# Token chunks of the second product taken from last to first, in a fused attention, experts and tanh-layer kernel on one core

## The chip, the cores and the metric

The kernel runs on one core of a Trainium2 chip. The metric is the time of one execution on the device in microseconds (us). In the profile, PE is TensorE (matrix products), PEld its weight loads, DVE is VectorE, ACT is ScalarE, POOL is GpSimd and SP is SyncE, which only issues DMAs here. Each of these engines takes its own instructions strictly in the order in which they stand in the program.

## The reference

Three layers follow one another; the output of one is the input of the next.

```python
# 1 attention: q, k, v are (2 batches, 8 heads, 576 positions, 64)
rel = pos[:, None] - pos[None, :]
mask_plain = (rel >= 0) & (rel < 32)                       # heads 0 to 3
mask_dil = (rel >= 0) & (rel < 128) & (rel % 4 == 0)       # heads 4 to 7
attn = softmax(where(mask, q @ k.T / sqrt(64), -1e9)) @ v
x = attn as (1152 tokens, 512)
# 2 four experts, all of them for every token
p = domain_probs / domain_probs.sum(-1)
for e in range(4):
    out += p[:, e:e + 1] * (relu(x @ w1[e]) @ w2[e])       # 512 -> 1024 -> 512
# 3 tanh layer, input: the out of layer 2
h = out @ w_in                                             # 512 -> 2048
out = (h - tanh(h)) @ w_out                                # 2048 -> 512
```

## The kernel before

**Precision.** A product of float32 numbers is made of three products of a faster 32-bit type: each operand is split into a high part, rounded by ACT, and a low part, the rest, by DVE or POOL. PE then adds high x high, high x low and low x high in PSUM.

**Stages and sets.** The hidden columns are cut into slices of 512: eight of the four experts (two each) and four of the tanh layer. The tokens are in two sets, set 0 of 512 tokens (four chunks of 128) and set 1 of 640 (five chunks). The list `seq` has 14 stages, each one slice with one or both sets. Stages 0 and 1 take set 0 alone, while the attention of set 1 is still being worked out beside them; stages 2 to 7 take both sets; stages 8 and 9 give set 1 the two slices that it missed; stages 10 (`N2`) to 13 (`LAST`) are the tanh layer with both sets.

**First product.** In stages 0 and 1 it is made directly (`whole`, L742, eight steps of 12 matmuls). From stage 2 on a scheme with seven products in place of eight is used, 14 steps of 6 matmuls for each stage and set (L803), listed in `ORDER`. Product P with its t (0 or 1) gives, after a few additions on DVE and POOL (L720), a half of one of the four hidden tiles `hts[g, f]`, f from 0 to 3: P2 gives half 0 of tile t, P3 half 1 of tile t, P7 half 1 of tile t + 2, and P4, the last, half 0 of tile t + 2. A half is half of the set's tokens: half 0 is the first 256 (or 320) of them.

**From product to hidden tile.** In expert stages ACT makes the high part with the relu (L723) and DVE the low part (L726). In tanh stages ACT takes the tanh (L774); for half 0 DVE subtracts, ACT makes the high part (L790) and DVE the low part (L128, into h); for half 1 DVE subtracts, ACT makes the high part (L165) and POOL the low part (L128, into h).

**Second product.** A chunk (`y_step`, L846) is 128 tokens x 512 outputs: for each f three matmuls, 12 in all, in one PSUM bank. `y_sum` then scales and adds it into `acc` (L867 in the experts, L876 in the tanh layer). Chunks are taken from the first tokens to the last. Before layer 3, `acc` is transposed on PE (L892).

**Order of the work.** The order is that in which the program emits the instructions, written out by hand. The list `steps` holds the products (`hs`) and chunks (`ys`) in PE's order; `start` gives each a scheduled time on a clock of its own. All other work is emitted through `when` and `later` with a due time on that clock. `merge(a, b, at)` puts the chunks `b` of the stage or set before between the products `a` at the places `at` (`FIRST`, `LATE` and `THEN`). `need(keys)` emits at once all work that is still pending under these keys; a chunk before asks for `("h", g)`, that is for all hidden tiles of its set.

**Other work in the stream.** Weights come by DMA and are split by ACT (L165) and POOL (L128). `w_in` and `w_out` are stored in another form and must be decoded by DVE, ACT, DVE and DVE again (L672, L676, L684, L689, with L683 on ACT), written back by DMA and loaded as weights later; 32 such decodes are spread by due times, nine of them in stages 11 and 12. The attention of set 1 is made during stages 0 to 2: scores on PE (L480), the masked maximum and the sums on DVE (L496, L502, L515 to L517), the multiplications on POOL (L503, L519), transposes on PE (L529, L542) and values on PE (L569); it is begun at due time 3 and repeated every `BEAT` = 11 for four pairs of heads; its result is then split into x operands (`prep`).

Of the kernel before, what the change touches and what calls it, by code (L numbers as in the profile page):

```python
# [26 lines left out]
SETS = [(0, 512), (512, 640)]  # L27
# [19 lines left out]
def _halves():  # L47
# [25 lines left out]
def tile_local_attention_moe_tanhshrink(  # L73
# [659 lines left out]
    def whole(n, f, half, kks=range(4)):  # L733
# [13 lines left out]
        if half == 1 and kks[-1] == 3:  # L747
            ht = hts[0, f] = h_tile(0)
            b, done = banks_.pop(f)
            later(0.0, lambda: relu(ht[:, 0], ht[:, 1], b, ("h", 0), done), ("h", 0))  # L750

# [13 lines left out]
    def hidden(n, g, f, half, b, done):  # L765

        Q = QH[g]
        hi, lo = (hts[g, f][:, i, half * Q:(half + 1) * Q] for i in range(2))
        key = ("h", g)
        if seq[n][0] < NS1:  # L770
# [22 lines left out]
    def product(n, g, P, t):  # L793
# [13 lines left out]

        later(0.0, lambda: sums_of(n, g, P, t, b, done), ("h", g))

    def sums_of(n, g, P, t, b, done):  # L810
# [19 lines left out]
        if P == 7:  # L830
            add(pt["u"], b, pt["u"])
        add(b, b, pt[{2: 1, 3: "u5", 7: "u5", 4: "u"}[P]])
        later(0.7, lambda: hidden(n, g, f, half, b, done), ("h", g))

    acc, oacc = {}, {}

    def y_step(n, g, c):

        need(("h", g), ("w2", n))
        y, done = f_bank()  # L840
        fs = range(NF)
        for f in fs:
            hh, hl = (hts[g, f][:, i, c * 128:(c + 1) * 128] for i in range(2))
            whi, wlo = (w2t[n, f][:, i] for i in range(2))
            for m, (a, b_) in enumerate(((hh, whi), (hh, wlo), (hl, whi))):
# [3 lines left out]
                )  # L849
        later(0.0, lambda: y_sum(n, g, c, y, done), ("y", n, g))  # L850

    def y_sum(n, g, c, y, done):
# [19 lines left out]
        else:  # L872
            k_ = 2 if n == LAST and ch == NCH - 1 else 1
            for i in range(k_):
# [50 lines left out]

    FIRST, LATE, THEN = (1, 2, 3, 4, 5), (4, 5, 6, 7, 8), (5, 7, 10, 13)
    steps = []
    for n in range(EARLY):
        steps += hs(n, 0) + ys(n, 0)
    steps += hs(EARLY, 0) + ys(EARLY, 0) + hs(EARLY, 1)  # L930
    for n in range(EARLY + 1, NS1):
        steps += merge(hs(n, 0), ys(n - 1, 1), FIRST) + merge(hs(n, 1), ys(n, 0), THEN)
    steps += ys(NS1 - 1, 1)
    for n in range(NS1, N2 - 1):
        steps += hs(n, 1) + ys(n, 1)
    steps += hs(N2 - 1, 1) + merge(hs(N2, 0), ys(N2 - 1, 1), LATE) + ys(N2, 0) + hs(N2, 1)
# [283 lines left out]
```

## Time and profile before

| | |
|---|---|
| median of 3 runs | 698.28 us (696.35 to 699.21) |
| the profiled execution | 698.15 us |
| its span, first to last instruction | 696.4 us |
| PE, DVE, POOL, ACT busy | 641.1, 452.2, 381.9, 291.7 us |
| mean granted clock of TensorE | 0.97 of full speed |
| matmuls | 4095 |

PE is busy for 92% of the span, the others for 42% to 65%. The profiled execution is 0.13 us under the median and lies between the runs, so its span can stand for the kernel; what it has beside the span is 1.75 us.

### The profile page before, as it was taken

How to read it: one execution, taken by the hardware profiler on the slowest of the kernel's cores; microseconds unless marked ns; L12 is line 12 of the kernel's file. 1: busy time of each engine (PE TensorE's matmuls, PEld its weight loads, DVE VectorE, ACT ScalarE, POOL GpSimd, SP SyncE). 2: the span in 40 equal slices, each digit the busy share in tenths (PEclk: the TensorE clock that was granted, in tenths of full speed). 3: DMA queues.
4: the chain of work that ended last, by engine and by line, in shares of the span. 5: the costliest groups of instructions: out<-in, count | busy, mean ns of one | idle time of the engine just before them, and what ended most of it. 6: DMA issues, size and time to landing. Idle time of an engine off the chain costs nothing.

```text
span 696.4 us, 10915 instructions
## 1 busy us (share of the span) xinstructions
PE 641.1 (92%) x4095; PEld 553.9 (80%) x4095; DVE 452.2 (65%) x859; ACT 291.7 (42%) x656; POOL 381.9 (55%) x352
## 2 busy tenths in 40 slices
PE   7876999999999999999999897999899968998997
PEld 3575878798888988978888787888698857986995
DVE  5575454655867867957948865754564883893662
ACT  2635545354433424324424444343674451652530
POOL 5466795373733814725625648584684860792520
PEclk9998999999999999999999999899999997998999
DMA  9951222003233234142151230523102233322012
GB/s 322 305 192 58 62 81 102 1 1 107 92 105 107 91 114 143 47 160 98 53 191 60 95 147 1 181 77 98 54 1 71 82 91 106 122 76 76 1 46 91
DMA packets 36693, 68.06 MB, mean 98 GB/s; under 512 B 4128, under 2 KB 10400, under 8 KB 36640
## 3 DMA queue, kind: packets, MB, share of 16 engines
q1 hardware_dynamic: 36640, 67.37, 28.9%
q8 instruction: 32, 0.52, 0.3%
q14 instruction: 21, 0.17, 0.1%
HBM read 56.61 MB, written 10.75 MB: 97 GB/s over the span
## 4 chain that ended last, share of the span: by engine, by line
PE 52%; DVE 24%; POOL 8%; issue 7%; DMA 4%; ACT 4%; SPq 0%; DVEq 0%; POOLq 0%; ACTq 0%
PE bank_f L846 21%; PE bank_f L803 12%; PE bank_s L846 8%; POOL w L128 4%; DVE h L726 3%; PE bank_a L846 3%; PE bank_s L803 3%; DVE single L689 3%; DVE single L676 2%; DVE single L684 2%; DVE single L672 2%; DMA double<-in_moe_w_out_dram 2%; DVE bank_f L720 2%; DMA in<-single 2%; PE bank_a L803 2%
## 5 line engine op out<-in xcount | busy, mean ns | idle before, releaser
L846 PE MATMUL bank_f<-w,h 128*128 128x512 f32 x876 | 223.2, 403 | 16.9 <-ACT h L790 8.0
L846 PEld LDWEIGHTS bank_f<-w,h 128*128 128x128 f32 x876 | 163.6, 193 | 56.4 <-ACT h L790 11.1
L128 POOL TENSOR_TENSOR w<-raw,w 128x512 fp32r<-128x512 f32 x110 | 145.2, 1326 | 108.3 <-ACT w L165 105.1
L803 PE MATMUL bank_f<-x,w 128*128 128x320 f32 (+1 forms) x1218 | 180.2, 300 | 4.4 <-DVE h L726 4.4
L803 PEld LDWEIGHTS bank_f<-x,w 128*128 128x128 f32 x1218 | 172.5, 191 | 10.2 <-DVE h L726 5.4
L720 POOL TENSOR_TENSOR sums<-u,p 128x320 f32<-128x320 f32 (+1 forms) x44 | 39.4, 899 | 97.0 <-DVE u L720 97.0
L846 PE MATMUL bank_s<-w,h 128*128 128x512 f32 x312 | 80.5, 408 | 5.6 <-ACT h L723 4.5
L165 ACT ACTIVATE w<-raw 128x512 fp32r<-128x512 f32 x112 | 68.7, 627 | 30.5 <-POOL raw L128 11.6
L846 PEld LDWEIGHTS bank_s<-w,h 128*128 128x128 f32 x312 | 60.0, 197 | 20.0 <-ACT h L723 5.4
L803 PE MATMUL bank_s<-x,w 128*128 128x320 f32 (+1 forms) x402 | 61.5, 298 | 1.5 <-DVE h L726 1.5
L803 PEld LDWEIGHTS bank_s<-x,w 128*128 128x128 f32 x402 | 57.2, 190 | 4.1 <-DVE h L726 2.2
L128 POOL TENSOR_TENSOR w<-sum,w 128x512 fp32r<-128x512 f32 x36 | 49.4, 1373 | 19.0 <-ACT w L165 19.0
L867 DVE SCALAR_TENSOR_TENSOR acc<-bank_f,pn,acc 128x512 f32<-128x512 f32 x43 | 32.1, 747 | 40.3 <-PE bank_f L846 40.0
L723 ACT ACTIVATE h<-bank_f 128x320 fp32r<-128x320 f32 (+2 forms) x83 | 35.0, 430 | 41.4 <-DVE bank_f L720 40.7
L726 DVE SCALAR_TENSOR_TENSOR h<-bank_f,h 128x320 fp32r<-128x320 f32 (+2 forms) x83 | 38.9, 474 | 13.7 <-ACT h L723 12.7
L683 ACT ACTIVATE double<-double 128x512 f32<-128x512 f32 x32 | 21.6, 676 | 56.7 <-DVE single L676 51.4
L676 DVE SCALAR_TENSOR_TENSOR single<-double,single 128x512 int32<-128x512 int32 x32 | 40.6, 1269 | 1.1
L815 ACT ACTIVATE p<-bank_f 128x320 f32<-128x320 f32 (+1 forms) x60 | 23.5, 418 | 37.7 <-PE bank_f L803 37.7
L165 ACT ACTIVATE w<-sum 128x512 fp32r<-128x512 f32 x36 | 22.7, 630 | 39.3 <-POOL sum L615 21.3
L689 DVE SCALAR_TENSOR_TENSOR single<-double,single 128x512 f32<-128x512 f32 x32 | 33.3, 1042 | 8.6 <-ACT double L683 7.9
L803 PE MATMUL bank_a<-x,w 128*128 128x320 f32 (+1 forms) x228 | 37.0, 298 | 1.0 <-DVE h L726 1.0
L803 PEld LDWEIGHTS bank_a<-x,w 128*128 128x128 f32 x228 | 33.3, 190 | 2.3 <-DVE h L726 1.3
(146 smaller groups left out, 838.0 us busy)
## 6 DMA issues: line engine op xcount, KB each, us to landing
raw<-in_moe_w_dram SPq DMA_DIRECT2D x40, 512.0 KB, 5.5
double<-in_moe_w_in_dram SPq DMA_DIRECT2D x16, 512.0 KB, 3.8
double<-in_moe_w_out_dram SPq DMA_DIRECT2D x16, 512.0 KB, 4.1
in<-single SPq DMA_DIRECT2D x16, 256.0 KB, 2.5
out<-single SPq DMA_DIRECT2D x16, 256.0 KB, 2.2
raw<-in SPq DMA_DIRECT2D x8, 512.0 KB, 5.6
raw<-out SPq DMA_DIRECT2D x8, 512.0 KB, 3.6
h<-in_v_dram SPq DMA_DIRECT2D x7, 512.0 KB, 8.6
```

Source lines behind the costliest of these rows:

```text
L128: engine.tensor_tensor(out=out, in0=a, in1=b, op=ALU.subtract)
L165: nc.scalar.activation(out=hi, in_=src, func=ACTF.Copy)
L676: nc.vector.scalar_tensor_tensor(out=t, in0=high, scalar=-0x40000000, in1=t, op0=ALU.bitwise_and, op1=ALU.bitwise_or)
L683: nc.scalar.activation(out=mag, in_=mag, func=ACTF.Square)
L689: nc.vector.scalar_tensor_tensor(out=w, in0=mag, scalar=HIGH_MIN * HIGH_MIN, in1=w, op0=ALU.is_ge, op1=ALU.mult)
L720: e.tensor_tensor(out=o, in0=x, in1=y, op=ALU.add)
L723: nc.scalar.activation(out=hi, in_=src, func=ACTF.Relu)
L726: nc.vector.scalar_tensor_tensor(out=lo, in0=src, scalar=0.0, in1=hi.bitcast(F32), op0=ALU.max, op1=ALU.subtract)
L803: nc.tensor.matmul(out=b, lhsT=w[:, wi, kk, t * 128:(t + 1) * 128], rhs=x[:, kk, xi, :], start=(kk == 0 and i == 0), stop=(kk == 1 and i = ...
L815: nc.scalar.activation(out=pt[P], in_=b, func=ACTF.Copy)
L846: nc.tensor.matmul(out=y, lhsT=a, rhs=b_, start=(f == 0 and m == 0), stop=(f == NF - 1 and m == 2),)
L867: nc.vector.scalar_tensor_tensor(out=t, in0=y, scalar=p, in1=t, op0=ALU.mult, op1=ALU.add)
```

## The change

1. **Chunks from the last tokens to the first.** `y_step` takes chunk 4 (or 3) first and chunk 0 last.
2. **A chunk asks only for the halves that it reads.** The pending work is filed under `("h", g, f, half)`, the fifth product's sum under `("u5", g, t)`.
3. **The first two chunks of a stage in two steps** (`direct`), in stages 0, 1, 2, 8 and 10. In stages 0 to 1 the first two chunks use f 0 to 2, and f 3 after both. In the other stages the first chunk's f 0 and 1 stand ahead of the last product; behind it come f 0 and 1 of the second chunk, and then f 2 and 3 of both.
4. **Places of chunks between products.** `LATE` goes from (4, 5, 6, 7, 8) to (3, 4, 5, 6, 8); in stages 12 and 13 (1, 2, 3, 4, 5) becomes (2, 3, 4, 5, 6).
5. **Decodes in stages 11 and 12.** Their stretch on the schedule's clock was the stage from 8 after its start to its end (39 of 47 in stage 11); now it is from 4 after its start to 8 before its end (35). Five decodes stand 7.0 apart in place of 7.8 in stage 11, and four 8.75 in place of 9.75 in stage 12; the first comes 4 earlier, the last some 7 earlier.
6. **Attention of set 1** begins at due time 9 in place of 3, with `BEAT` 10.5 in place of 11.

```diff
+MAKES = {
+    1: lambda t: (), 5: lambda t: (), 6: lambda t: (), 2: lambda t: (t, 0), 3: lambda t: (t, 1),
+    7: lambda t: (t + 2, 1), 4: lambda t: (t + 2, 0),
+}
...
-        key = ("h", g)
+        key = ("h", g, f, half)
...
-        later(0.0, lambda: sums_of(n, g, P, t, b, done), ("h", g))
+        later(0.0, lambda: sums_of(n, g, P, t, b, done), ("h", g, *MAKES[P](t)))
...
-    def y_step(n, g, c):
-
-        need(("h", g), ("w2", n))
-        y, done = f_bank()
-        fs = range(NF)
+    def y_step(kind, n, g, i):
+        c = SETS[g][1] // 128 - 1 - i
+        first = 3 if n < EARLY else 2
+        fs = {"y": range(NF), "ya": range(first), "yb": range(first, NF)}[kind]
+        if n < EARLY:
+            need(*[("h", g, f) for f in fs])
+        else:
+            halves = {c * 128 // QH[g], (c * 128 + 127) // QH[g]}
+            need(*[("h", g, f, half) for f in fs for half in halves])
+        need(("w2", n))
+        y, done = opened.pop((g, c)) if kind == "yb" else f_bank()
+        if kind == "ya":
+            opened[g, c] = y, done
...
-    FIRST, LATE, THEN = (1, 2, 3, 4, 5), (4, 5, 6, 7, 8), (5, 7, 10, 13)
+    def direct(h, n, g):
+
+        cs = ys(n, g)
+        (a0, b0), (a1, b1) = [[(kind, *step[1:]) for kind in ("ya", "yb")] for step in cs[:2]]
+        if n < EARLY:
+            return h + [a0, a1, b0, b1] + cs[2:]
+        return h[:-1] + [a0] + h[-1:] + [a1, b0, b1] + cs[2:]
+
+    FIRST, LATE, THEN = (1, 2, 3, 4, 5), (3, 4, 5, 6, 8), (5, 7, 10, 13)
...
-        steps += hs(n, 0) + ys(n, 0)
-    steps += hs(EARLY, 0) + ys(EARLY, 0) + hs(EARLY, 1)
+        steps += direct(hs(n, 0), n, 0)
+    steps += direct(hs(EARLY, 0), EARLY, 0) + hs(EARLY, 1)
...
-        steps += hs(n, 1) + ys(n, 1)
-    steps += hs(N2 - 1, 1) + merge(hs(N2, 0), ys(N2 - 1, 1), LATE) + ys(N2, 0) + hs(N2, 1)
+        steps += direct(hs(n, 1), n, 1)
+    steps += hs(N2 - 1, 1) + direct(merge(hs(N2, 0), ys(N2 - 1, 1), LATE), N2, 0) + hs(N2, 1)
...
-        first = FIRST if n > N2 + 1 else LATE
+        first = (2, 3, 4, 5, 6) if n > N2 + 1 else LATE
...
-            a += 8.0
+            a, b = a + 4.0, b - 8.0
...
-    BEAT = 11.0
+    BEAT = 10.5
...
-        due = 3.0 + BEAT * n
+        due = 9.0 + BEAT * n
...
-        when(BEAT * 3 + 20.0 + 4.0 * c, lambda c=c: prep(1, c, True, nc.vector, nc.gpsimd), ("x", 1, False))
+        when(BEAT * 3 + 25.0 + 3.0 * c, lambda c=c: prep(1, c, True, nc.vector, nc.gpsimd), ("x", 1, False))
```

The numbers of instructions do not change. Lines move a little: L742 is L747 in the changed kernel, L803 is L809, L846 is L865, L529 is L534, L480 is L485, L876 is L896, L672, L676, L684 and L689 are L677, L681, L689 and L694, L720 is L725, and L128 is L133.

**PE at the end of stage 0, before.** `w` and `h` with their numbers are the second weights and the hidden tiles of f 0 to 3 in this order; `att` is the second set's attention.

```order
L742 MATMUL bank_f<-x_532,w_226 128x256 x6
L529 MATMUL bank_a<-ident,att 96x128 x4
L846 MATMUL bank_f<-w_622,h_637 128x512 x3
L846 MATMUL bank_f<-w_638,h_702 128x512 x3
L846 MATMUL bank_f<-w_680,h_750 128x512 x3
L846 MATMUL bank_f<-w_703,h_798 128x512 x3
L529 MATMUL bank_a<-ident,att 96x128 x4
L480 MATMUL bank_s<-x_151,x_145 64x96 x20
```

The same place in the changed kernel:

```order
L747 MATMUL bank_f<-x_532,w_226 128x256 x6
L865 MATMUL bank_f<-w_622,h_637 128x512 x3
L865 MATMUL bank_f<-w_638,h_676 128x512 x3
L865 MATMUL bank_f<-w_658,h_717 128x512 x3
L865 MATMUL bank_f<-w_622,h_637 128x512 x3
L865 MATMUL bank_f<-w_638,h_676 128x512 x3
L865 MATMUL bank_f<-w_658,h_717 128x512 x3
L865 MATMUL bank_f<-w_677,h_777 128x512 x6
L865 MATMUL bank_f<-w_622,h_637 128x512 x3
L865 MATMUL bank_f<-w_638,h_676 128x512 x3
L865 MATMUL bank_f<-w_658,h_717 128x512 x3
L865 MATMUL bank_f<-w_677,h_777 128x512 x3
L534 MATMUL bank_a<-ident,att 96x128 x4
```

The transposes of the attention (L529) stood between the last product and the first chunk, and again behind it; now three whole chunks stand ahead of the first of them, and 18 matmuls ahead of the first use of the fourth hidden tile.

**PE at the end of stage 8, before.** L803 is the end of the first product; `h_0_1` to `h_3_1` are the four hidden tiles of set 1.

```order
L803 MATMUL bank_f<-x_1585,w_4294 128x320 x12
L846 MATMUL bank_s<-w_4441,h_0_1_4515 128x512 x3
L846 MATMUL bank_s<-w_4462,h_1_1_4528 128x512 x3
L846 MATMUL bank_s<-w_4477,h_2_1_4516 128x512 x3
L846 MATMUL bank_s<-w_4501,h_3_1_4529 128x512 x3
```

The same place in the changed kernel:

```order
L809 MATMUL bank_f<-x_1618,w_4307 128x320 x6
L865 MATMUL bank_f<-w_4441,h_0_1_4515 128x512 x3
L865 MATMUL bank_f<-w_4462,h_1_1_4528 128x512 x3
L809 MATMUL bank_s<-x_1618,w_4307 128x320 x6
L865 MATMUL bank_s<-w_4441,h_0_1_4515 128x512 x3
L865 MATMUL bank_s<-w_4462,h_1_1_4528 128x512 x3
L865 MATMUL bank_f<-w_4477,h_2_1_4516 128x512 x3
L865 MATMUL bank_f<-w_4501,h_3_1_4529 128x512 x3
```

Six matmuls of the first chunk stand ahead of the last product, which is six of the former twelve, and six of the second chunk between it and the tiles f 2 and f 3.

**DVE at the end of stage 11, before.** L720 and L128 into `bank` or `h` make the hidden tiles f 2 and f 3 of set 1, half 0; L876 adds a chunk; L672, L676, L684 and L689 are one decode.

```order
L672 TENSOR_SCALAR single<-double 128x512
L676 SCALAR_TENSOR_TENSOR single<-double,single 128x512
L876 TENSOR_TENSOR acc<-bank_f,acc 128x512
L684 SCALAR_TENSOR_TENSOR single<-double,single 128x512
L128 TENSOR_TENSOR h_2_1_5829<-bank_a,h_2_1_5829 128x320
L720 TENSOR_TENSOR bank_f<-bank_f,u 128x320
L689 SCALAR_TENSOR_TENSOR single<-double,single 128x512
L128 TENSOR_TENSOR bank_f<-bank_f,sums 128x320
L128 TENSOR_TENSOR h_3_1_5860<-bank_f,h_3_1_5860 128x320
```

The same place in the changed kernel:

```order
L896 TENSOR_TENSOR acc<-bank_f,acc 128x512
L133 TENSOR_TENSOR h_2_1_5836<-bank_a,h_2_1_5836 128x320
L725 TENSOR_TENSOR bank_f<-bank_f,u 128x320
L133 TENSOR_TENSOR bank_f<-bank_f,sums 128x320
L133 TENSOR_TENSOR h_3_1_5869<-bank_f,h_3_1_5869 128x320
L896 TENSOR_TENSOR acc<-bank_f,acc 128x512
L896 TENSOR_TENSOR acc<-bank_s,acc 128x512
L677 TENSOR_SCALAR single<-double 128x512
L681 SCALAR_TENSOR_TENSOR single<-double,single 128x512
```

The decode stood ahead of the low parts of the last two tiles; now they stand ahead of a decode. On PE at this place one product of the next stage stood ahead of the first chunk, and two stand there now.

## Rows read from the trace of the kernel before

**Rows 1.** The page: PE's busy time; the granted clock in 40 slices, in tenths.

```profile
PE 641.1 (92%) x4095; PEld 553.9 (80%) x4095; DVE 452.2 (65%) x859; ACT 291.7 (42%) x656; POOL 381.9 (55%) x352
...
PEclk9998999999999999999999999899999997998999
```

**Rows 2.** Windows: length, PE PEld DVE ACT POOL busy, granted clock, DMA share, GB/s.

```profile
41.50:134.60 93.10, 80.94 (x740) 69.43 (x737) 56.82 (x109) 44.21 (x97) 60.53 (x57) 0.96 0.21 68
...
427.37:440.00 12.63, 8.80 (x27) 6.64 (x26) 7.72 (x14) 4.37 (x10) 8.91 (x7) 0.73 0.03 4
489.88:498.08 8.20, 6.54 (x28) 4.50 (x26) 4.51 (x9) 4.97 (x14) 7.08 (x8) 1.00 0.19 64
566.48:584.18 17.70, 9.62 (x34) 7.06 (x33) 10.77 (x20) 5.64 (x13) 7.70 (x7) 0.71 0.47 149
625.45:638.10 12.65, 9.62 (x32) 7.12 (x31) 5.67 (x10) 4.20 (x10) 3.97 (x4) 0.73 0.32 105
```

**Rows 3.** Windows of four stretches at half clock, same columns.

```profile
53.30:60.00 6.70, 2.92 (x9) 2.51 (x10) 6.36 (x14) 4.44 (x11) 3.27 (x4) 0.50 0.07 26
432.20:438.90 6.70, 6.15 (x15) 4.77 (x16) 5.66 (x10) 2.06 (x4) 3.90 (x4) 0.50 0.00 0
572.10:582.20 10.10, 5.37 (x16) 4.18 (x16) 6.16 (x10) 2.71 (x6) 2.17 (x2) 0.50 0.45 139
630.10:636.90 6.80, 5.64 (x16) 4.75 (x17) 1.68 (x3) 1.20 (x4) 0.12 (x1) 0.50 0.47 149
```

**Rows 4.** Timeline of PE: start, length, instruction, idle time before and its releaser.

```profile
57.08 1.09 PE L529 MATMUL bank_a<-ident,att 128*96 128x128 f32 x4 [8.13 <-POOL att L519]
...
134.63 1.62 PE L803 MATMUL bank_f<-x,w 128*128 128x320 f32 x10
```

**Rows 5.** Timeline of DVE in stages 0 and 1.

```profile
47.04 0.65 DVE L496 SCALAR_TENSOR_TENSOR att<-bank_s,mask_True 128x480 f32<-128x480 f32 x1
...
57.23 0.68 DVE L726 SCALAR_TENSOR_TENSOR h<-bank_f,h 128x512 fp32r<-128x512 f32 x1
...
130.51 0.48 DVE L128 TENSOR_TENSOR x<-xf,x 128x320 fp32r<-128x320 f32 x1
```

**Rows 6.** Timeline of PE, stages 3 to 6: first and last of four waits.

```profile
200.00 1.03 PE L846 MATMUL bank_a<-w,h 128*128 128x512 f32 x3 [0.70 <-ACT h L723]
...
348.97 1.03 PE L846 MATMUL bank_s<-w,h 128*128 128x512 f32 x3 [0.70 <-ACT h L723]
```

**Rows 7.** Timeline of DVE at the end of stage 8.

```profile
430.13 0.49 DVE L726 SCALAR_TENSOR_TENSOR h<-bank_f,h 128x320 fp32r<-128x320 f32 x1 [3.17 <-ACT h L723]
```

**Rows 8.** Timeline of PE from the end of stage 11 on.

```profile
575.20 0.79 PE L846 MATMUL bank_f<-w,h 128*128 128x512 f32 x1 [3.09 <-DVE h L128]
...
580.36 3.83 PE L846 MATMUL bank_s<-w,h 128*128 128x512 f32 x12
584.02 0.87 PE L803 MATMUL bank_s<-x,w 128*128 128x256 f32 x6
...
588.19 2.91 PE L846 MATMUL bank_f<-w,h 128*128 128x512 f32 x12
590.94 0.88 PE L803 MATMUL bank_f<-x,w 128*128 128x256 f32 x6
591.65 0.63 PE L846 MATMUL bank_f<-w,h 128*128 128x512 f32 x2
```

**Rows 9.** Timeline of POOL: low parts of hidden tiles at the ends of stages 11 and 12.

```profile
571.95 1.04 POOL L128 TENSOR_TENSOR h<-x,h 128x320 fp32r<-128x320 f32 x1
...
627.68 1.31 POOL L128 TENSOR_TENSOR h<-x,h 128x320 fp32r<-128x320 f32 x1
```

**Rows 10.** The decodes: two on DVE's timeline, then the tile's durations, min/median/max in ns.

```profile
561.40 0.67 DVE L672 TENSOR_SCALAR single<-double 128x512 int32<-128x512 int32 x1 [1.69 <-DMA in<-single]
...
571.50 0.78 DVE L672 TENSOR_SCALAR single<-double 128x512 int32<-128x512 int32 x1 [0.84 <-DMA in<-single]
...
L676 DVE SCALAR_TENSOR_TENSOR single<-double,single x32: 691/1658/1669, 149.8 to 623.2; 128x512 int32<-128x512 int32 x32
```

More of the change, by code (lines that the diff above doesn't have):

```diff
@@ L749, in whole @@
             b, done = banks_.pop(f)
-            later(0.0, lambda: relu(ht[:, 0], ht[:, 1], b, ("h", 0), done), ("h", 0))
+            key = ("h", 0, f)
+            later(0.0, lambda: relu(ht[:, 0], ht[:, 1], b, key, done), key)
     store, ring = [], {"u5": 0, "th": 0}
@@ L821, in sums_of @@
             add(u, b, pt[1])
-            later(0.5, lambda: add(u5, u, p5, nc.gpsimd), ("h", g, t, "u5"))
+            later(0.5, lambda: add(u5, u, p5, nc.gpsimd), ("u5", g, t))
             done()
             return
-        f, half = {2: (t, 0), 3: (t, 1), 7: (t + 2, 1), 4: (t + 2, 0)}[P]
+        f, half = MAKES[P](t)
         if P == 2:
@@ L828, in sums_of @@
         if P in (3, 7):
-            need(("h", g, t, "u5"))
+            need(("u5", g, t))
         if P == 7:
@@ L832, in sums_of @@
         add(b, b, pt[{2: 1, 3: "u5", 7: "u5", 4: "u"}[P]])
-        later(0.7, lambda: hidden(n, g, f, half, b, done), ("h", g))
+        later(0.7, lambda: hidden(n, g, f, half, b, done), ("h", g, f, half))
     acc, oacc = {}, {}
-    def y_step(n, g, c):
-        need(("h", g), ("w2", n))
-        y, done = f_bank()
-        fs = range(NF)
+    opened = {}
+    def y_step(kind, n, g, i):
[11 more added lines that the diff above has]
+            opened[g, c] = y, done
         for f in fs:
@@ L849, in y_step @@
                 )
-        later(0.0, lambda: y_sum(n, g, c, y, done), ("y", n, g))
+        if kind != "ya":
+            later(0.0, lambda: y_sum(n, g, c, y, done), ("y", n, g))
     def y_sum(n, g, c, y, done):
@@ L872, in y_sum @@
         else:
-            k_ = 2 if n == LAST and ch == NCH - 1 else 1
+            k_ = 2 if n == LAST and g == 1 and c == 0 else 1
             for i in range(k_):
@@ L944, in duration @@
             return 2.73
+        if kind in ("ya", "yb"):
+            return 2.73 * ((3 if n < EARLY else 2) if kind == "ya" else (1 if n < EARLY else 2)) / 4
         if n < EARLY:
@@ L951, in tile_local_attention_moe_tanhshrink @@
         start[step] = END
+        if step[0] == "yb":
+            start[("y", *step[1:])] = END + duration(*step) - 2.73
         END += duration(*step)
     def emit_step(kind, n, g, i):
-        if kind == "y":
-            y_step(n, g, i)
+        if kind[0] == "y":
+            y_step(kind, n, g, i)
         elif n < EARLY:
```

## The prediction

> **What bounds the kernel now.** I read the page first, for which engine is full: PE is busy 641.1 of 696.4 us of span, the others far less, and its clock dips in single slices only [rows 1]. So PE's work sets the time, and since the change neither adds nor removes an instruction, all that it can win is PE's idle time and PE's work at half clock. Then PE's waits, and a window around each: five stretches hold most of what the change touches [rows 2]. PE is idle there for 93.10 - 80.94 = 12.16 us (stages 0 and 1 and what follows), 3.83 (end of stage 8), 1.66 (start of stage 10), 8.08 (end of stage 11) and 3.03 (end of stage 12). In four of them the granted clock fell to 0.50, the lower of its two levels, after or in an idle time, and PE did 2.92, 6.15, 5.37 and 5.64 us of its work so [rows 3]. The rate without waits is seen in a chunk at full clock: 590.94 - 588.19 = 2.75 us for 12 matmuls, 0.229 each, and 591.65 - 590.94 = 0.71 for a product of set 0 [rows 8]. What a stretch loses is its length less its work at these prices.
>
> **Stages 0 and 1.** After stage 0's last product PE waits 8.13 us in front of the attention's transposes, for POOL [rows 4]; behind them stands the first chunk. In the changed order the chunk comes first and waits for the low part of f 2, which DVE ends at 57.23 + 0.68 = 57.9 [rows 5]. From before that instruction DVE loses two maskings of 0.65 [rows 5], two reductions of the same size, estimated as long, and a sum with its two small followers, estimated at 1.0: 3.6 together, so f 2 is ready at 54.3. PE is free at 57.08 - 8.13 = 48.95, and waits 5.3. The 18 matmuls that come next (4.1 us) cover f 3. Idle time and half clock lose 12.16 + 2.92/2 = 13.6 now; 8.3 is won, and I take 0.8 off because the clock may still fall after 5.3 idle: **-7.5**. Best case -13.6. Worst case: the attention's end moves later in order, and set 1's x operand is its last link. DVE ends it at 130.51 + 0.48 = 131.0 [rows 5], and set 1's products start at 134.63 [rows 4], a margin of 3.6. Its last part is due 2.5 later (56.5 + 3 against 53 + 4). If this chain doesn't come ahead with PE, all but 1.1 of the gain is waited away: -1.1. POOL is busy 60.53 of 93.10 in this window [rows 2], so the chain has room to come ahead.
>
> **Stages 3 to 6.** Four waits of 0.70 for the relu of the last half [rows 6]. The chunk that comes first now reads half 1, which the last product doesn't make: **-2.8** (best -2.8, worst half of it, -1.4).
>
> **Stage 8.** The 24 matmuls from 427.37 to 440.00 would take 5.5 at the full rate; 7.1 is lost. The first six now go ahead of the last product (estimated at 0.88 from 0.71 by its 320 columns), from 426.5 on. But the high part of f 1 comes only at 430.1, where DVE's wait for it ends [rows 7]; ACT is what is late, not the product's place. So PE waits some 2.9 after f 0, and then has 0.69 + 0.88 + 4.1 to do: 435.8, at best -4.2. If the 18 matmuls run at half clock as now, 4.1 of that goes: -0.1. Between the two I take **-2.3**.
>
> **Stage 10.** From 489.88 to 498.08 the two first chunks take 8.20 [rows 2], 2.7 more than 24 matmuls. Their f 2 and 3 now come behind 12 matmuls that need neither; an estimated 0.4 is left: **-2.3** (best -2.7, worst 0).
>
> **End of stage 11.** From 566.48 to 584.02 PE does 24 matmuls and a product, 6.2 us; 17.54 - 6.2 = 11.3 is lost. One of its waits, 3.09, is for the low part of a half 0 [rows 8], behind decode steps of up to 0.78 and 1.66 on DVE [rows 10]. The new first chunk reads half 1 alone, whose last low part POOL ends at 571.95 + 1.04 = 573.0 [rows 9]. PE, with one more product ahead and nine matmuls of f 0 to 2, gets there at 566.48 + 0.71 + 2.06 = 569.25; two of the three matmuls of f 3 don't need the low part, so 3.75 - 0.46 = 3.3 of wait stays. 11.3 - 3.3 = 8.0, less 1.0 for a few matmuls at half clock: **-7.0**. Best -11.3; worst -3, if only the product (0.71) and the decode's two steps (2.4) are won.
>
> **End of stage 12.** The same: 12.65 - 6.2 = 6.4 is lost. POOL's low part ends at 627.68 + 1.31 = 629.0 [rows 9], PE gets there at 625.45 + 2.77 = 628.2; 0.3 stays, and 0.6 for the clock: **-5.5** (best -6.4; worst, by the share 3.0 of 8.0 of the stage before, -2.3).
>
> **Other places.** The keys and the split of the last chunk move a few tenths: **-0.5** (best -1.5; worst +0.6, because the chunk that is summed last is now the one that is transposed first).
>
> **Decodes.** They cost DVE the same work; their place behind the tiles is counted above. Price of the closer spacing: two start 571.50 - 561.40 = 10.1 apart now, and DVE stood 0.84 and 1.69 for the DMA of the one before [rows 10]. Such a wait hides as long as PE has products whose sums come later, and gets longer if decodes come every 7.0. **+2.0**, an estimate of some 0.2 for each of nine; best 0. The second decode step takes 0.69 at least and 1.66 in the median [rows 10], so at worst nine go from the short to the long: 9 x 0.97 = +8.7.
>
> The Trainium skill (SBUF - State Buffer, "Who interferes with whom") says that a DVE instruction with two inputs in SBUF and a GpSimd instruction that reads SBUF exclude each other for their whole length. That second step has both inputs in SBUF, and the trace agrees that it has two lengths; that the page's lock is the cause, no row here shows. By the rule, decodes moved beside POOL's weight splits would all be slow, as in the fifth rival below.
>
> **Sum.** -7.5 - 2.8 - 2.3 - 2.3 - 7.0 - 5.5 - 0.5 + 2.0 = -25.9, against the profiled execution's 698.15 us (0.13 below the median of the runs): **672**. All bounds at their best -42.4 or 656; all at their worst +1.4 or 699.6.
>
> **Rivals.**
> 1. Set 1's x operand becomes the wait, at 127 to 134: early term -1.1, time 672.2 + 6.4 = 679. For it: the later due. Against: POOL's idle 32.6 in the window. Chance 0.13.
> 2. POOL's low parts hold the first chunks of stages 12 and 13's turn as long as DVE and ACT did: those two terms at their worst, + 7.2, time 679. For it: half 1 goes through POOL alone, behind its weight splits; against: both rows end before PE's present waits do. Chance 0.14.
> 3. All waits and half clocks at these places go: 656. Against: rows 7 name ACT for stage 8, which the change leaves. Chance 0.08.
> 4. DVE's decodes become a chain through the DMA: 5 x (10.1 - 7.0) + 4 x (10.1 - 8.75) = 20.9 in place of 2.0, time 691. For it: DVE waits for that DMA already. Against: 10.1 holds schedule time stretched by PE's own waits, and the waits were 1.69 and 0.84 only. Chance 0.07.
> 5. The moved decodes' second steps all take the long form: +8.7 in place of 2.0, 679. Against: the median shows that most do so already. Chance 0.04.
> 6. Slower: in the tanh stages the first chunk of every set (eight of them) now reads half 1 through POOL, where it read half 0 through DVE. If each waits there, the 14.8 of stages 10 to 12 isn't won (687), and from 11.1/8 = 1.4 per place on the kernel is slower; with two of POOL's 1.31 in front of each it is 687 + 21 = 708. Against: POOL is busy 7.70 of 17.70 and 3.97 of 12.65 there [rows 2], far from full. Chance 0.04.
> 7. The waits only move, each to the next instruction that needs the same tile: about 698. Against: in stages 11 and 12 the tiles themselves are ready earlier. Chance 0.04.
>
> **How the numbers follow.** The forecast as worked out has 0.46. The range of 660 to 688 holds it and rivals 1, 2 and 5, and 1 and 2 together (686); rivals 4, 6 and 7 and most of 3 are left out, 0.2 or a little more. A change of 0.5%, 3.5 us, is about what a measurement of this kernel tells from none: faster 0.92, within it 0.04 (rival 7), slower 0.04 (rival 6).
>
> **What the changed profile would show.** PE's first gap after stage 0's last product some 5 us and released by DVE's low part of a hidden tile, no longer by POOL's attention; set 1's first products near 127. No 0.70 waits in stages 3 to 6. At the end of stage 8 a wait of about 3 before f 1, for ACT. At the ends of stages 11 and 12 one wait each, of 3 and under 1 us, for POOL's low part of half 1, and shorter stretches at half clock. Wrong would be: a new wait in front of set 1's first products, waits for POOL in front of many chunks of stages 10 to 13, or chunk sums and tiles on DVE behind a decode that waits for its DMA.

## The result, and the profile after

The changed kernel takes 675.91 us (median of 4 runs, 675.24 to 676.62) against 698.36 for the kernel before in the same runs: a ratio of 0.9683, 95% interval 0.9658 to 0.9707. The forecast was 672 with a range of 660 to 688. The profiled execution took 675.24 us, its span is 673.5. The page's same two rows as in [rows 1]:

```profile
PE 632.2 (94%) x4095; PEld 550.5 (82%) x4095; DVE 452.7 (67%) x859; ACT 289.9 (43%) x656; POOL 381.0 (57%) x352
...
PEclk8898999999999999999999999989999999999999
```

PE does the same 4095 matmuls in 8.9 us less busy time and waits 14 us less. The other engines do the same work as before. That the sum came out is partly luck, and the next table shows where. Both programs run the same number of matmuls, so the start of PE's n-th matmul can be read in both traces; at numbers where the same work lies behind, the difference of two such starts is the time of a stretch. Stage 11, for instance, begins near matmul 3120 (504.17 before, 489.78 after), and its end near 3486 (566.12 and 556.80). The last columns are experiments that are told below; all but the first are in us against the profiled execution of before, and a minus is won. Each column is one profiled execution.

| stretch (matmuls) | before | forecast | changed | order only | order + keys | old places | old dues | wide decodes |
|---|---|---|---|---|---|---|---|---|
| stages 0 to 2 (360 to 1140) | 94.4 | -7.5 | -9.7 | 0.0 | -1.3 | -9.8 | -9.8 | -9.7 |
| stages 3 to 6 (1500 to 2460) | 172.4 | -2.8 | -4.2 | -4.0 | -4.2 | -4.2 | -4.2 | -4.2 |
| transposes before layer 3 (2460 to 2640) | 37.3 | in -0.5 | -4.0 | +0.5 | -4.0 | -4.0 | -4.0 | -4.0 |
| end of stage 8 (2760 to 2820) | 20.1 | -2.3 | -3.9 | -2.7 | -2.8 | -1.1 | -2.6 | -2.5 |
| stage 9, start of 10 (2820 to 2964) | 24.8 | 0 | +7.4 | +4.3 | +4.3 | +5.0 | +6.7 | +0.5 |
| first chunks of stage 10 (3060 to 3120) | 16.1 | -2.3 | +0.4 | +1.6 | +4.3 | +0.4 | +0.4 | +1.2 |
| stage 11 (3120 to 3486) | 61.9 | +1.1 | +5.1 | +1.0 | 0.0 | +5.0 | 0.0 | +1.8 |
| end of stage 11 (3486 to 3600) | 31.5 | -7.0 | -7.8 | -5.0 | -5.9 | -5.3 | -7.9 | -7.8 |
| stage 12 (3600 to 3760) | 27.2 | +0.9 | +1.2 | -0.5 | -0.5 | +2.5 | -0.5 | -0.5 |
| end of stage 12 (3760 to 3870) | 26.2 | -5.5 | -6.5 | -4.8 | -4.8 | -6.0 | -5.4 | -5.5 |
| all (last matmul's end) | 692.6 | -25.9 | -22.9 | -10.5 | -15.2 | -17.9 | -27.7 | -30.9 |

Nearly every gain is larger than forecast, and stages 9 and 11 give 12.5 us back. (The +2.0 of the decodes stands in the rows of stages 11 and 12, by five and four of nine; the rows left out hold -0.9 us in the changed kernel.)

**Stages 0 to 2.** PE's timeline of the changed kernel, to set beside [rows 4]:

```profile
50.20 0.51 PE L865 MATMUL bank_f<-w,h 128*128 128x512 f32 x1 [0.34 <-DVE h L731]
51.78 0.74 PE L865 MATMUL bank_f<-w,h 128*128 128x512 f32 x2 [1.08 <-ACT h L728]
52.98 8.08 PE L865 MATMUL bank_f<-w,h 128*128 128x512 f32 x28 [0.47 <-DVE h L731]
60.90 0.60 PE L534 MATMUL bank_a<-ident,att 128*96 128x128 f32 x4
...
124.64 3.53 PE L809 MATMUL bank_f<-x,w 128*128 128x320 f32 x23
```

The wait of 8.13 us for POOL is gone. What stays is 0.34 + 1.08 + 0.47 for hidden tiles, and three chunks are done before the first transposes of the attention at 60.90. Set 1's products start at 124.64 in place of 134.63, with no wait for their x operand. Two of the windows of [rows 2] have their counterpart here:

```profile
48.53:61.30 12.77, 10.88 (x42) 7.97 (x40) 11.03 (x20) 7.28 (x15) 9.29 (x10) 0.87 0.14 42
...
558.24:567.75 9.51, 7.57 (x32) 5.23 (x33) 6.21 (x14) 5.26 (x13) 6.67 (x7) 1.00 0.60 195
```

The first is the end of stage 0; part of it still ran at half clock (0.87 in the mean): 28 matmuls took 8.08 us, 0.289 each against 0.229. The second is the end of stage 11: no half clock, and two chunks in 9.5 us that took 17.7.

**Stages 8 and 9.** PE, then DVE, in the changed kernel:

```profile
411.91 1.02 PE L865 MATMUL bank_f<-w,h 128*128 128x512 f32 x3 [2.81 <-ACT h L728]
...
431.78 1.14 PE L809 MATMUL bank_f<-x,w 128*128 128x320 f32 x6 [0.43 <-DVE acc L887]
434.23 5.31 PE L809 MATMUL bank_f<-x,w 128*128 128x320 f32 x24 [1.31 <-DVE acc L887]
...
445.12 0.74 PE L809 MATMUL bank_f<-x,w 128*128 128x256 f32 x4 [1.04 <-POOL w L133]
447.98 4.38 PE L865 MATMUL bank_f<-w,h 128*128 128x512 f32 x11 [2.13 <-DVE h L731]
...
418.33 0.74 DVE L887 SCALAR_TENSOR_TENSOR acc<-bank_f,pn,acc 128x512 f32<-128x512 f32 x1
...
426.75 0.43 DVE L677 TENSOR_SCALAR single<-double 128x512 int32<-128x512 int32 x1 [4.59 <-issue]
427.21 0.69 DVE L681 SCALAR_TENSOR_TENSOR single<-double,single 128x512 int32<-128x512 int32 x1
427.82 0.74 DVE L887 SCALAR_TENSOR_TENSOR acc<-bank_a,pn,acc 128x512 f32<-128x512 f32 x1
...
430.99 0.74 DVE L887 SCALAR_TENSOR_TENSOR acc<-bank_f,pn,acc 128x512 f32<-128x512 f32 x1
```

At 411.91 stands the wait that was forecast (2.9 for ACT's relu, 2.81 measured). The rest was not. A decode's first step (L677) holds DVE for 4.59 us; the profile names no releaser, but the DMA that writes the decode before, issued at 422.57, lands at 426.67. Behind that step, in DVE's order, stands the chunk sum of 427.82, whose PSUM bank had been full for long. Sums run late until 433.44, and PE, which is now some 4 us ahead, waits for banks at 431.78 and 434.23. The third decode also stands ahead of stage 10's weights on ACT, and PE waits for those at 445.12. Of the 7.4 us, some 3.8 are longer waits. Nearly all of the rest, some 3.4 by the starts of the matmuls, is half clock behind these waits: the kernel before passed the same stretch at 1.00, and in the changed one the clock fell in two places, behind the waits for banks and behind those for weights and a tile. The windows of the stretch before, and of the two places after:

```profile
446.44:471.21 24.77, 23.30 (x146) 21.66 (x144) 15.85 (x29) 11.23 (x27) 20.04 (x17) 1.00 0.27 87
```

```profile
432.00:437.00 5.00, 3.69 (x18) 3.43 (x18) 4.31 (x9) 4.13 (x10) 2.86 (x2) 0.79 0.61 202
447.00:453.00 6.00, 5.02 (x17) 4.06 (x18) 4.14 (x10) 3.90 (x11) 4.54 (x4) 0.72 0.00 0
```

With the new order of the chunks alone the stretch loses 4.3. No wait for a chunk sum stands there; PE waits 0.94 us for a weight and 2.13 for a tile, and some 2.9 of the loss is half clock behind them (0.64 from 456 to 465).

**Stage 11.** The same, with the cause named, on DVE, ACT, POOL and PE (the first PE row is from stage 10, the last from the end of stage 11):

```profile
525.42 0.43 DVE L677 TENSOR_SCALAR single<-double 128x512 int32<-128x512 int32 x1 [5.28 <-DMA out<-single]
...
526.66 0.68 ACT L688 ACTIVATE double<-double 128x512 f32<-128x512 f32 x1 [6.04 <-DVE single L681]
...
479.80 0.73 PE L865 MATMUL bank_f<-w,h 128*128 128x512 f32 x2 [1.96 <-POOL w L133]
...
528.23 0.98 PE L809 MATMUL bank_a<-x,w 128*128 128x256 f32 x6 [2.23 <-DVE h L133]
...
529.36 2.56 POOL L133 TENSOR_TENSOR w<-raw,w 128x512 fp32r<-128x512 f32 x2 [10.83 <-ACT w L170]
...
538.33 0.73 PE L865 MATMUL bank_s<-w,h 128*128 128x512 f32 x2 [2.09 <-POOL w L133]
...
545.39 0.43 DVE L677 TENSOR_SCALAR single<-double 128x512 int32<-128x512 int32 x1 [5.24 <-DMA in<-single]
...
555.34 2.69 PE L809 MATMUL bank_f<-x,w 128*128 128x320 f32 x18 [1.01 <-DVE sums L133]
...
563.78 0.50 PE L865 MATMUL bank_f<-w,h 128*128 128x512 f32 x1 [1.10 <-POOL h L133]
```

DVE stands 5.28 us for the DMA that writes out the decode before; ACT's part of the decode waits for DVE, ACT's weight parts stand behind it, POOL's behind those; PE waits 2.23 us for a tile behind the decode and 2.09 for a weight, and at 555.34 another 1.01 for a sum behind one more decode. Not every such wait costs time: a decode stands 5.24 us for its DMA at 545.39, and PE runs on without a wait from 540.66 to 555.34.

### The profile page after: what moved, and what is told of

The parts are those of the page before. It is cut to its first block, busy times and chain, and to the rows that moved or that the text cites. A ratio compares the mean times of both kernels' runs of the same rounds, so it can differ in the third digit from the quotient of the medians.

```text
span 673.5 us, 10926 instructions
## 1 busy us (share of the span) xinstructions
PE 632.2 (94%) x4095; PEld 550.5 (82%) x4095; DVE 452.7 (67%) x859; ACT 289.9 (43%) x656; POOL 381.0 (57%) x352
## 4 chain that ended last, share of the span: by engine, by line
PE 67%; DVE 12%; POOL 8%; issue 6%; DMA 3%; ACT 3%; SPq 0%; DVEq 0%; POOLq 0%; ACTq 0%
PE bank_f L865 25%; PE bank_f L809 17%; PE bank_s L865 9%; PE bank_s L809 5%; POOL w L133 4%; PE bank_a L865 3%; PE bank_a L809 3%; DMA in<-single 2%; DVE single L694 2%; DVE h L731 2%; PE bank_a L574 1%; DVE single L689 1%; PE bank_f L1133 1%; DMA out<-single 1%; DVE u L725 1%
## 5 line engine op out<-in xcount | busy, mean ns | idle before, releaser
L865 PE MATMUL bank_f<-w,h 128*128 128x512 f32 x888 | 221.7, 398 | 10.9 <-ACT h L728 3.9
L133 POOL TENSOR_TENSOR w<-raw,w 128x512 fp32r<-128x512 f32 x110 | 146.1, 1334 | 114.9 <-ACT w L170 114.2
L865 PEld LDWEIGHTS bank_f<-w,h 128*128 128x128 f32 x888 | 164.5, 191 | 47.1 <-ACT h L728 4.6
L809 PE MATMUL bank_f<-x,w 128*128 128x256 f32 (+1 forms) x1212 | 180.8, 301 | 7.0 <-DVE h L731 3.2
L809 PEld LDWEIGHTS bank_f<-x,w 128*128 128x128 f32 x1212 | 171.7, 191 | 13.8 <-DVE h L731 4.0
L725 POOL TENSOR_TENSOR sums<-u,p 128x320 f32<-128x320 f32 (+1 forms) x44 | 39.5, 903 | 83.8 <-DVE u L725 83.8
L865 PE MATMUL bank_s<-w,h 128*128 128x512 f32 x300 | 73.1, 392 | 2.5 <-POOL w L133 2.1
L865 PEld LDWEIGHTS bank_s<-w,h 128*128 128x128 f32 x300 | 55.0, 188 | 14.1 <-POOL w L133 2.5
L809 PE MATMUL bank_s<-x,w 128*128 128x320 f32 (+1 forms) x408 | 62.8, 298 | 2.8 <-DVE h L731 1.5
L809 PEld LDWEIGHTS bank_s<-x,w 128*128 128x128 f32 x408 | 58.1, 189 | 5.8 <-DVE h L731 2.2
L133 POOL TENSOR_TENSOR w<-sum,w 128x512 fp32r<-128x512 f32 x36 | 48.8, 1355 | 17.0 <-ACT w L170 17.0
L681 DVE SCALAR_TENSOR_TENSOR single<-double,single 128x512 int32<-128x512 int32 x32 | 41.0, 1282 | 1.1
L809 PE MATMUL bank_a<-x,w 128*128 128x320 f32 (+1 forms) x228 | 37.1, 298 | 3.3 <-DVE h L133 2.2
L694 DVE SCALAR_TENSOR_TENSOR single<-double,single 128x512 f32<-128x512 f32 x32 | 31.9, 997 | 8.4 <-ACT double L688 7.6
L809 PEld LDWEIGHTS bank_a<-x,w 128*128 128x128 f32 x228 | 33.3, 189 | 4.8 <-DVE h L133 2.4
L677 DVE TENSOR_SCALAR single<-double 128x512 int32<-128x512 int32 x32 | 22.3, 698 | 17.3 <-DMA in<-single 7.4
```

What stands on the lines that cost most here:

```text
L133: engine.tensor_tensor(out=out, in0=a, in1=b, op=ALU.subtract)
L677: nc.vector.tensor_scalar(out=t, in0=high, scalar1=3, scalar2=0x3FFFFFFF, op0=ALU.logical_shift_left, op1=ALU.bitwise_and,)
L681: nc.vector.scalar_tensor_tensor(out=t, in0=high, scalar=-0x40000000, in1=t, op0=ALU.bitwise_and, op1=ALU.bitwise_or)
L694: nc.vector.scalar_tensor_tensor(out=w, in0=mag, scalar=HIGH_MIN * HIGH_MIN, in1=w, op0=ALU.is_ge, op1=ALU.mult)
L725: e.tensor_tensor(out=o, in0=x, in1=y, op=ALU.add)
L809: nc.tensor.matmul(out=b, lhsT=w[:, wi, kk, t * 128:(t + 1) * 128], rhs=x[:, kk, xi, :], start=(kk == 0 and i == 0), stop=(kk == 1 and i = ...
```

## The experiments

All times are medians; ratios are against runs of the kernel before that were measured beside each experiment, whose median lay between 698.5 and 700.1 us, so the ratios compare better than the times.

**Order and keys alone.** Two-step chunks (in all five stages), places, decodes and attention go back; the core of it:

```diff
-        steps += direct(hs(n, 1), n, 1)
+        steps += hs(n, 1) + ys(n, 1)
...
-    FIRST, LATE, THEN = (1, 2, 3, 4, 5), (3, 4, 5, 6, 8), (5, 7, 10, 13)
+    FIRST, LATE, THEN = (1, 2, 3, 4, 5), (4, 5, 6, 7, 8), (5, 7, 10, 13)
...
-            a, b = a + 4.0, b - 8.0
+            a += 8.0
...
-    BEAT = 10.5
+    BEAT = 11.0
```

> The kernel before with points 1 and 2 of the change alone: chunks from last to first, keys by half; one-step chunks, places, decodes and attention as before. Theory A (that a first chunk doesn't need the last product, and doesn't flush what stands pending behind it, wins most of what is won after stage 2): the four waits in stages 3 to 6 go (4.2 us by the two traces), the transposes before layer 3 lose their wait (4.0), and the ends of stages 11 and 12 win about half of what they won (6 of 13): 682 to 686 us. Theory B (these gains come from the two-step chunks, the moved places and the moved decodes): 692 to 696 us, with only the four waits gone.

Measured: 683.63 us, ratio 0.9778 (0.9754 to 0.9801). Theory A holds, and with more at the ends of stages 11 and 12 than the half that it gave them: 5.9 of 7.8 and 4.8 of 6.5 (table).

**Order alone.** As above, and a chunk again asks for everything of its set:

```diff
-            halves = {c * 128 // QH[g], (c * 128 + 127) // QH[g]}
-            need(*[("h", g, f, half) for f in fs for half in halves])
+            need(*[("h", g, f, half) for f in range(NF) for half in range(2)])
+            need(*[("u5", g, t) for t in range(2)])
```

> The kernel before with point 1 alone: chunks from last to first, every other instruction of each engine in its place of before. Theory A (a first chunk of half 1 doesn't wait for the last product's half; the refined keys are needed only to move the transposes before layer 3 behind a chunk): the four waits of stages 3 to 6 go (4.2 us) and the ends of stages 11 and 12 shorten as in the run with keys (about 10), but the transposes keep their wait: 4 less gain than with the keys, 12 to 10 us below the kernel before in the same call. Theory B (without the keys the pending work is still emitted ahead of the chunk, so nothing is won): within 2 us of the kernel before.

Measured: 685.98 us (683.52 to 687.98), ratio 0.9815 (0.977 to 0.9861), 12.5 us below. Theory A. Each engine's instructions stand in the order of before, only that the chunks read other tokens; so the four waits of stages 3 to 6 and most of the ends of stages 11 and 12 are won by that alone. The transposes before layer 3 keep their wait:

```profile
393.41 0.89 PE L912 MATMUL bank_s<-ident,acc 128*128 128x128 f32 x4 [2.60 <-DVE acc L887]
```

In the kernel with the keys the first transposes stand behind set 1's first chunk, and PE doesn't wait in front of them (timeline of the changed kernel):

```profile
380.74 2.91 PE L865 MATMUL bank_f<-w,h 128*128 128x512 f32 x12
383.52 0.66 PE L912 MATMUL bank_s<-ident,acc 128*128 128x128 f32 x4
383.93 3.01 PE L865 MATMUL bank_f<-w,h 128*128 128x512 f32 x12
```

So the keys are worth 4.5 us at one place: a chunk that asked for the whole set had the pending transposes emitted ahead of it. At other places they win and lose: 1.3 us in stages 0 to 2 and about 1 each in stage 11 and at its end are won, and 2.7 are lost in the first chunks of stage 10 (+4.3 against +1.6). The intervals of the two ratios overlap, so the times do not tell what the keys are worth in sum. The changed kernel loses only 0.4 in those chunks of stage 10, and no more with the old places or the old due times, which leaves the two-step chunks as what helps there.

**Old attention.**

```diff
-    BEAT = 10.5
+    BEAT = 11.0
...
-        due = 9.0 + BEAT * n
+        due = 3.0 + BEAT * n
```

(and the last x parts at `BEAT * 3 + 20.0 + 4.0 * c` again.)

> The changed kernel with the second set's attention begun as early as before. Theory A (PE's wait of 8.1 us in stage 0 was made by the attention's place in front of the first chunk; two-step chunks alone don't move it): 681 to 684 us, with the wait for POOL back at 57. Theory B (the two-step chunks fill the time in any order): 676 to 678 us.

Measured: 683.98 us, ratio 0.9778 (0.9762 to 0.9794). The size is Theory A's, its mechanism only in part: the wait for POOL doesn't come back, but the first chunk waits for hidden tiles behind the attention's work on DVE:

```profile
53.07 0.80 PE L865 MATMUL bank_f<-w,h 128*128 128x512 f32 x1 [3.01 <-DVE h L731]
54.72 1.22 PE L865 MATMUL bank_f<-w,h 128*128 128x512 f32 x2 [0.85 <-ACT h L728]
57.61 0.80 PE L865 MATMUL bank_f<-w,h 128*128 128x512 f32 x1 [1.68 <-DVE h L731]
```

**One-step chunks in stages 0 to 2**, with the attention later:

```diff
-        steps += direct(hs(n, 0), n, 0)
-    steps += direct(hs(EARLY, 0), EARLY, 0) + hs(EARLY, 1)
+        steps += hs(n, 0) + ys(n, 0)
+    steps += hs(EARLY, 0) + ys(EARLY, 0) + hs(EARLY, 1)
```

> The changed kernel with one-step chunks in stages 0, 1 and 2; the second set's attention stays later. Theory A (the attention's place makes 7.6 of the 9.7 us won there, two-step chunks the other 2.1): 1.5 to 3 us over the changed kernel, 20 to 21 below the kernel before. Theory B (each needs the other, since the run with the old attention and two-step chunks kept 7.5 of the loss): 6 to 9 us over the changed kernel, 14 to 17 below the kernel before.

Measured: 678.87 us, ratio 0.9721 (0.9684 to 0.9759). By the ratios that is 2.7 us over the changed kernel: Theory A. In stages 0 to 2 it wins 6.5 of the 9.7 us, of which the order and keys alone make 1.3; the two-step chunks make the last 3.2.

**One-step chunks in stage 8.**

```diff
-        steps += direct(hs(n, 1), n, 1)
+        steps += hs(n, 1) + ys(n, 1)
```

> The changed kernel with one-step chunks in stage 8 alone. Theory A (the two-step chunks of stage 8 bring PE 3.9 us ahead of three decodes on DVE, and a decode that waits there for its DMA holds the chunk sums behind it and so PSUM banks, weights and PE in stage 9, which loses 7.9): without them stage 8 is 3.9 longer and stage 9 up to 7.9 shorter, 671 to 673 us, and PE has no wait for a chunk sum in stage 9. Theory B (stage 9 loses by the moved places of its last chunks, and stage 8's gain is real): 679 to 681 us, with the waits of stage 9 still there.

Measured: 672.88 us, ratio 0.9618 (0.9602 to 0.9635). Stage 9 and the start of stage 10 lose 3.0 in place of 7.4, and no wait for a chunk sum is left in stage 9; those for weights and tiles at its end stay (0.85 and 2.12), and the first chunks of stage 10 lose 0.9 and stage 11 2.0 more. So the loss is where Theory A put it, but its first step is wrong: two-step chunks don't bring PE ahead in stage 8. That stage wins 2.6 here in place of 3.9, and the difference is the clock's: the kernel with both repairs (below) has one-step chunks too and wins 4.1, with the clock at 1.00 from 410 to 416; the one with old due times has two-step chunks and wins 2.6, with 0.72 in the same window. The order of the chunks brings PE ahead; the two-step chunks only put the first chunk's sum later on DVE, from 415.61 here to 418.33 in the changed kernel, and the decodes and other sums with it. DVE's row here:

```profile
415.61 0.75 DVE L887 SCALAR_TENSOR_TENSOR acc<-bank_s,pn,acc 128x512 f32<-128x512 f32 x1
```

**Old due times of the decodes in stages 11 and 12.**

```diff
-            a, b = a + 4.0, b - 8.0
+            a += 8.0
```

> The changed kernel with the decodes of stages 11 and 12 at their due times of before. Theory A (the closer decodes wait for each other's DMA and hold DVE, ACT and the weights behind them: 5.0 us lost in stage 11 and 2.0 in stage 12): most of the 7 comes back, and up to 4 of it is lost where a decode again stands ahead of the last tiles, 669 to 674 us. Theory B (the move of the decodes is what shortens the ends of stages 11 and 12): these lengthen by 5 to 8, 679 to 684 us.

Measured: 670.34 us, ratio 0.9583 (0.9567 to 0.9598). The loss in stages 11 and 12 is gone (5.1 and 1.7 us), the end of stage 11 wins as much as with the moved decodes (-7.9), and only the end of stage 12 gives up 1.0. The moved decodes cost 6.8 us and won 1.0.

**Old places of the chunks.**

```diff
-        first = (2, 3, 4, 5, 6) if n > N2 + 1 else LATE
+        first = FIRST if n > N2 + 1 else LATE
```

(and `LATE` as before.)

> The changed kernel with the places of before for the chunks between products (point 4 undone). Theory A (of the 8.2 and 7.1 us won at the ends of stages 11 and 12, the order of the chunks makes 5.9 and 4.8, and the later places the other 2.3 and 1.3 to 2.3; the moved decodes make next to nothing of the first): the two stretches win 5 to 6.5 and 4 to 5.5, the rest as in the changed kernel, 18 to 20 us below the kernel before in the same call. Theory B (the moved decodes make that part): both stretches as in the changed kernel, 22 to 24 below.

Measured: 680.02 us, ratio 0.9717 (0.9677 to 0.9757), 17.9 by the traces. The end of stage 11 wins 5.3 and that of stage 12 6.0, both less than in the changed kernel. Theory A for stage 11; in stage 12 the places make 0.5 only, and 1.3 us more are lost ahead of it.

**Both repairs: one-step chunks in stage 8 and old due times.** The diffs of the two runs together.

> The changed kernel with one-step chunks in stage 8 and the decodes of stages 11 and 12 at their old due times, both that won alone (3.1 us in stages 8 and 9, and 4.8). Theory A (two places, two causes): the gains add, 30 to 32 us below the kernel before in the same call. Theory B (time won in stage 9 is lost again at a decode later): 27 to 29 below it.

Measured: 668.57 us, ratio 0.9568 (0.9534 to 0.9602), 30 us below, 28.9 by the traces: between the theories. By the traces the 4.8 us that the old due times win in the changed kernel, and the 3.1 that the one-step chunks win in stages 8 and 9, miss their sum by some 2. Stages 8 and 9 are not the place: together they lose 0.5 here (4.6 - 4.1) and 0.4 with the one-step chunks alone (3.0 - 2.6). What this kernel loses and the one with the old due times alone does not stands later: 1.6 us at the turn from stage 10 to stage 11, where the clock falls, and 1.0 at the end of stage 11, in a wait for a sum behind a decode. The second is of the kind that Theory B expected. The next run has both losses too, and its rows are shown there.

**Decodes around stage 8 further apart**, old due times in stages 11 and 12, two-step chunks kept:

```diff
-            where += [start["y", NS1, 1, 0] - 4.0 + 4.0 * i for i in range(3)]
+            where += [start["y", NS1, 1, 0] - 4.0 + 8.0 * i for i in range(3)]
```

> The changed kernel with old due times of the decodes in stages 11 and 12, two-step chunks kept in stage 8, and the three decodes around stage 8 due 8 apart in place of 4. Theory A (the second decode's wait for the DMA of the first holds chunk sums on DVE and weights on ACT): PE has no wait for a chunk sum in stage 9, its wait for POOL's weights shrinks, and 3 to 6 of the 7 us lost in stages 9 and 10 come back: 31 to 34 below the kernel before. Theory B (stage 9 is held by POOL's weight splits, wherever the decodes stand): 27 to 29 below it.

Measured: 665.71 us (663.57 to 667.45), ratio 0.9518 (0.947 to 0.9565), the fastest median of the study, though the interval overlaps that of the kernel with both repairs. Theory A: the first step of the second decode no longer waits, and the chunk sum ahead of it waits only for PE. Of this kernel, DVE's and PE's timeline:

```profile
425.36 0.75 DVE L887 SCALAR_TENSOR_TENSOR acc<-bank_f,pn,acc 128x512 f32<-128x512 f32 x1 [1.63 <-PE bank_f L865]
426.03 0.42 DVE L677 TENSOR_SCALAR single<-double 128x512 int32<-128x512 int32 x1
...
444.66 3.02 PE L865 MATMUL bank_f<-w,h 128*128 128x512 f32 x12 [1.85 <-DVE h L731]
```

Stage 9 and the start of stage 10 lose 0.5 in place of 6.7 us, and the clock stays up there (1.00 from 426.5 to 450). Of the 6.2 us won, 2.6 are lost later, 0.8 in stage 10 and 1.8 in stage 11. That is not a longer wait for weights: the waits for POOL's weights there are the same with the old due times alone (1.95 there and 1.94 here, 1.19 in both). Some 1.6 are half clock: both kernels wait about 1.45 us for ACT in front of the last transposes of stage 10, and here the clock falls behind it (0.62 from 483.0 to 487.5) and there it stays at 1.00. The other 1.0 is a wait for a sum on DVE, behind a decode that waits 1.87 us for a DMA (545.01); with the old due times alone that decode waits 1.90, but PE gets to the sum after it is ready. The chunk behind the transposes, with the old due times alone and here, and then PE's wait for the sum:

```profile
488.63 3.02 PE L865 MATMUL bank_s<-w,h 128*128 128x512 f32 x12 [0.16 <-ACT x2f L916]
```

```profile
482.68 4.48 PE L865 MATMUL bank_s<-w,h 128*128 128x512 f32 x12 [0.15 <-ACT x2f L916]
...
548.08 2.10 PE L809 MATMUL bank_f<-x,w 128*128 128x320 f32 x14 [0.73 <-DVE sums L133]
```

## Why the prediction was right, and where not

**What bounds the kernel** was right: PE's idle time and half clock were all that could be won. **Stages 0 and 1:** forecast -7.5, measured -9.7. The mechanism was right, the wait of 5.3 us too long, for two reasons. The working counts all the time from PE's last product to f 2's low part as lost, but eight matmuls that don't need this part stand in it (the rows at 48.53, 50.20 and 51.78 above): 1.8 us of work at 0.229. And the low part starts on DVE at 52.25 in place of 57.23, so it is ready at 52.9 and not at 54.3. DVE works without a gap ahead of it in both kernels, from 45.6 and 45.3 on. The rows of the attention that no longer stand there held 3.5 us, about what I took; some 1.2 more come from DVE's other rows, which are shorter now. One of them before, and the same one after with the low part behind it:

```profile
56.10 1.21 DVE L128 TENSOR_TENSOR xf<-xf 128x256 f32<-128x256 f32 x1
```

```profile
51.91 0.41 DVE L133 TENSOR_TENSOR xf<-xf 128x256 f32<-128x256 f32 x1
52.25 0.68 DVE L731 SCALAR_TENSOR_TENSOR h<-bank_f,h 128x512 fp32r<-128x512 f32 x1
```

POOL is busy beside most of the longer row and not beside the shorter one; that this is the reason is argued. Rival 1 was wrong: x came ahead with PE.

**Stages 3 to 6:** forecast -2.8, measured -4.2, because I priced these four by the idle time of the row (0.70), and elsewhere by the length of the stretch less its work. The latter gives 1.05 for each: behind the row's idle time the first matmul starts 1.08 us after the one ahead of it and the next two 0.34 and 0.29 apart, where 0.23 is usual.

**Other places:** the -0.5 was the step that failed in kind. I gave the keys "a few tenths" without looking at what a chunk's demand drags ahead of it. They are worth 4.5 us at the transposes, as the runs of order alone and order with keys show.

**Stage 8:** the wait for ACT came as forecast, and -3.9 is near the best case of the estimate, with the clock up. In seven other kernels, in which it fell, this stretch wins 1.1 to 2.8, about the middle that I took. But the reason was wrong: it is the order, and not the first six matmuls ahead of the last product, that wins here.

**Stage 10:** -2.3 forecast, +0.4 measured. I had the tiles as the limit. What PE waits for at 479.80 is a second weight from POOL (1.96 us), which nothing in the change brings sooner.

**Ends of stages 11 and 12:** -7.0 and -5.5, measured -7.8 and -6.5; the waits for POOL's low part are there (1.10 at the first), no half clock came. One reason was wrong: that the decode stands behind the tiles now made no difference at stage 11, since the old due times win as much. The order of the chunks and their places do. Rivals 2 and 6 were wrong.

**Decodes:** +2.0 forecast, and the losses that they make are 5.1 + 1.7 us in stages 11 and 12 and some 6 in stage 9, half clock behind the waits included (6.2 come back where the three decodes stand 8 apart). This is rival 4's mechanism. I had put its price at 20.9 us and its chance at 0.07, and looked for it in stages 11 and 12 only. The three decodes around stage 8 don't move in the change, so I gave them no term; but PE moved against them, and half clock behind new waits there had no price either. By the table the gains came out some 11 us larger than forecast, and the losses, stage 10 among them, some 14: the sum was 3 us off because the errors went both ways.

The Trainium skill (SBUF - State Buffer, "Who interferes with whom") gave rival 5. The trace agrees with the rule: in the kernel before, no POOL instruction runs beside any of the 11 second decode steps that took about 0.7 us, and one runs for half to all of each of the 21 that took 1.1 us or more; after the change it is 12 and 20. So every case fits the rule, and the change moved only one step from the long kind to the short: rival 5 did not come.

What stays open is the buffer. In the code, decodes share a pool of four buffers, two of which are held through the tanh layer, so each decode must wait for the write of one before. A fifth buffer would test that by itself; it wasn't tried.

## What to carry to other kernels

Let the first consumer read the half that doesn't depend on the last producer: reversing the order of the chunks, with no instruction moved, won 10.5 us here by the traces. When one engine is brought ahead, look on every in-order engine for work that waits for a DMA (2.1 to 6.2 us from issue to landing for the decodes here), and for what stands behind it; a step that isn't touched by the change can still be the largest loss (7.4 us in stage 9), and half clock behind a new wait can be nearly half of it. Price a wait by the length of its stretch less the work at the full rate, and not by the idle time of one row.

## What the runs showed that was not expected

The lengths of one DVE instruction, about 0.69 us or 1.1 to 1.67, sort without exception by whether POOL was busy beside it (above). And the same wait doesn't always bring the half clock: at the end of stage 8 PE waited 2.81 us in the changed kernel and the clock stayed at 1.00; in the kernel with wide decodes it waited 2.80 us at the same instruction, and part of the stretch ran at half clock. The windows of both, in this order:

```profile
408.25:421.00 12.75, 9.94 (x47) 7.92 (x46) 8.96 (x17) 4.96 (x10) 10.15 (x9) 1.00 0.01 1
```

```profile
408.80:421.50 12.70, 9.90 (x40) 8.12 (x39) 8.70 (x16) 5.32 (x11) 9.76 (x9) 0.87 0.00 1
```

This moves the stretch by 1 to 3 us from one kernel to the next. The wait of about 1.45 us in stage 10 is a second such case, worth 1.6 us. What decides it, no run here shows; so a difference of this size between two traces needs a look at the clock before it is put down to a change.
